# Sync-queue DMAs of an attention backward pass chained in traced order, with a third buffer for stored dV

## The chip, the cores and the metric

One core of a Trainium2 chip runs the whole program. The metric is device time in microseconds (us), the median of several executions. A ratio is the mean time of one kernel's runs over the mean of the other kernel's runs of the same rounds, so it is not quite the ratio of the medians that are quoted beside it.

## The reference, cut to what matters

Two independent blocks A and B each do attention of 96 queries on a cache of 512 keys and values, for 8 batches and 32 heads of width 128, in bf16. What is wanted is the output and the gradients of all inputs.

```python
def _A_ref(x, k_cache, v_cache, wq, wo):           # B=8, Sq=96, D=640, H=32, Sk=512, Dh=128
    q = (x @ wq).reshape(B, Sq, H, Dh).transpose(0, 2, 1, 3)
    scores = jnp.einsum("bhqd,bhkd->bhqk", q, k_cache) * (Dh ** -0.5)
    p = softmax(scores)
    o = jnp.einsum("bhqk,bhkd->bhqd", p, v_cache)
    return o.transpose(0, 2, 1, 3).reshape(B, Sq, H * Dh) @ wo
# ... B the same; concatenate([a, b], -1); then jax.vjp with grad_out for all ten inputs
```

For the argument it is enough that the kernel, for every (block, head, batch), reads K and V twice, once transposed and once as they lie, and writes a dK and a dV of the same size.

## The kernel before

The kernel is a software pipeline written by hand. One *tick* is one (head, batch). Each stage of the work is put on a list with a tick and a slot; the list is sorted and traced in that order. The framework's scheduler then orders the instructions of every engine by priority and readiness, so an engine's order can differ from the traced one.

Heads go in pairs (`HP = 2`): one DMA moves the K (or V, dK, dV) of two heads of one batch, 256 KB. There are 256 such *pairs*, one every two ticks, and each has six DMAs, all issued from the sync engine (SP): two transposing loads, two plain loads, two stores. The transposing loads are traced for two batches at once (`TB = 2`). I call the batches of such a couple *even* and *odd*.

```python
OFF = dict(t=-1, kn=3, vn=0, s2=3, s3=3, s4=4, s5=5, s6=6, s7=7, s8=8)
HP = 2
TB = 2
# ...
    def p_ldT(h, b, which):                       # transposing load of K (0) or V (1)
        def f():
            t_ = kvp.tile([128, F4 * KC, 16], BF16, name=key + "_p", bufs=(4 if which == 0 else 6))
            # ...
            nc.sync.dma_start_transpose(t_[:], src)                              # L246
    # p_ldn: plain load into K_sb / V_sb, bufs=4                                   L257
    def p_st(h, b, which):                        # store of dV (1) or dK (0)
        def f():
            t_ = CS[(blk, h, b)]["dV_p" if which == 1 else "dK_p"]
            dst = (dv if which == 1 else dk)[b, h:h + HP]
            nc.sync.dma_start(dst.rearrange("h (p c) d -> p h (c d)", c=KC), t_[:])   # L266
    # ...
    def c_s4(h, b):                               # dV = P^T dO, then a copy out of PSUM
        def f():
            # ... four matmuls into dV_ps
            if j == 0:
                st["dV_p"] = wk.tile([128, HP, KC * 128], BF16, name="dV_sb", bufs=2)
            nc.scalar.activation(dV_p[:, j], dV_ps[:], ACT.Identity, scale=1.0)  # L362
    # c_s7: the same for dK: dK_sb, bufs=2, copy on ScalarE                        L428
    # ...
                if j == 0:
                    if b % TB == 0:
                        for which in (0, 1):
                            for bb in range(b, b + TB):
                                em.add(ct + OFF["t"], SLOTS["LOAD"] - 1, p_ldT(h, bb, which))
                    em.add(ct + OFF["kn"], SLOTS["LOAD"], p_ldn(h, b, 0))
                    em.add(ct + OFF["vn"], SLOTS["LOAD"], p_ldn(h, b, 1))
                    em.add(ct + HP + OFF["s4"], SLOTS["LOAD"], p_st(h, b, 1))
                    em.add(ct + HP + OFF["s7"] + 1, SLOTS["LOAD"], p_st(h, b, 0))
```

## Time and profile before

Time 1757.6 us (three runs, 1757.0 to 1759.6).

| | before |
|---|---|
| TensorE (PE) busy | 1643 us, 93% |
| gaps between PE's instructions, summed (with the 6 us before the first) | 110 us |
| mean granted TensorE clock | 0.984 |
| DMA engines busy, all queues (87.7 + 8.4 + 0.7 + 0.1% of the span) | 1708 us of 1763 |
| ScalarE (ACT) copies waiting for a store, dK_sb / dV_sb | 24.5 / 23.3 us |

These lines are from the page of the kernel before. DMA is a row of 40 slices of the span in tenths; q1 is the sync queue and q0 the one issued by GpSimd, with packets, MB and share of the time of the 16 DMA engines; the last two lines are groups of instructions: count, busy us, mean ns, idle time just before them and what ended most of it.

```profile
span 1763.2 us, 59487 instructions
...
PE 1643.4 (93%) x22474; PEld 1371.8 (78%) x22648; DVE 1392.3 (79%) x3597; ACT 1349.2 (77%) x3529; POOL 712.9 (40%) x1306
...
DMA  9999999999999999999999999999999999999983
...
q1 hardware_dynamic: 304672, 404.75, 87.7%
q0 software_dynamic: 15648, 49.83, 8.4%
...
L428 ACT ACTIVATE dK_sb<-dK_ps 128x512 bf16<-128x512 f32 x512 | 302.6, 591 | 108.9 <-PE dK_ps L423 70.4
L362 ACT ACTIVATE dV_sb<-dV_ps 128x512 bf16<-128x512 f32 x512 | 307.8, 601 | 26.0 <-DMA out_dram<-dV_sb 23.3
```

TensorE and the DMA engines are both nearly full. The views that tell where PE loses time are the waits (total us, times, longest):

```profile
ACT dK_sb L428 <- DMA out_dram<-dK_sb: 24.5, 20, 3.3
...
ACT dV_sb L362 <- DMA out_dram<-dV_sb: 23.3, 16, 3.3
...
PE S_ps L286 <- ACT dK_sb L428: 18.1, 13, 3.3
```

A ScalarE copy into dK_sb or dV_sb sometimes finds its buffer still being stored (20 and 16 times); PE then waits for the copy, which empties a PSUM buffer (18.1 us at S_ps). The timeline of the sync queue (start, us, instruction) shows the order that the scheduler makes of one pair's six DMAs:

```profile
522.04 1.16 SPq L246 DMA_TRANSPOSE VT_p<-in_A_v_cache_dram  x1
523.29 0.53 SPq L266 DMA_DIRECT2D out_dram<-dV_sb  x1
523.91 1.82 SPq L246 DMA_TRANSPOSE KT_p<-in_A_k_cache_dram  x1
525.83 0.53 SPq L257 DMA_DIRECT2D V_sb<-in_A_v_cache_dram  x1
526.46 0.42 SPq L266 DMA_DIRECT2D out_dram<-dK_sb  x1
526.97 0.42 SPq L257 DMA_DIRECT2D K_sb<-in_A_k_cache_dram  x1
```

Transposes come in twos, often with a store between them, and a dK store is issued 2.4 us (median over the trace) after its data is ready. I call this time its *lag*.

### The profile page before, as it was taken

The numbers are of one execution on the slowest core, as the hardware profiler recorded it, in microseconds if no ns is written. First come the engines' busy times: TensorE is split into PE (matmuls) and PEld (weight loads), VectorE is DVE, ScalarE is ACT, GpSimd is POOL, SyncE is SP. The second block draws the span as 40 slices with busy tenths as digits, with TensorE's granted clock in tenths as the row PEclk, the third lists the DMA queues.
The fourth block names the chain that finished last, engine by engine and source line by source line (L and its number), as shares of the span: only waits on it lengthen the run. The fifth ranks groups of instructions, "written<-read, shape, count | busy, mean of one in ns | idle before, by whom it ended". The sixth has DMA issues, their size and how long they took to land. (4 is left out here: it accounts for less than half of the span.)

```text
span 1763.2 us, 59487 instructions
## 1 busy us (share of the span) xinstructions
PE 1643.4 (93%) x22474; PEld 1371.8 (78%) x22648; DVE 1392.3 (79%) x3597; ACT 1349.2 (77%) x3529; POOL 712.9 (40%) x1306
## 2 busy tenths in 40 slices
PE   5899989999999999998998999999999989999997
PEld 4787878788888888786886787877878878787776
DVE  4786868878888888887886778787888878888885
ACT  4888967878778787875876898786787867878782
POOL 3343434433433443434365344343443334343336
PEclk9899999999999999999999999999999999999999
DMA  9999999999999999999999999999999999999983
GB/s 267 262 280 258 265 251 262 270 261 273 266 266 284 264 268 257 273 271 259 242 278 282 262 268 273 249 268 252 264 265 269 262 239 265 267 269 246 263 249 111
DMA packets 320609, 458.39 MB, mean 260 GB/s; under 512 B 37216, under 2 KB 300896, under 8 KB 312128
## 3 DMA queue, kind: packets, MB, share of 16 engines
q1 hardware_dynamic: 304672, 404.75, 87.7%
q0 software_dynamic: 15648, 49.83, 8.4%
q8 instruction: 177, 2.90, 0.7%
q14 instruction: 112, 0.92, 0.1%
HBM read 161.09 MB, written 159.12 MB: 182 GB/s over the span
## 5 line engine op out<-in xcount | busy, mean ns | idle before, releaser
L298 ACT ACTIVATE E_sb<-S_ps,negm 96x512 bf16<-96x512 f32 x512 | 349.2, 682 | 212.6 <-DVE negm L288 203.6
L317 POOL TENSOR_SCALAR P_sb<-E_sb,rinv 96x512 bf16<-96x512 bf16 x512 | 354.2, 692 | 343.8 <-DVE rinv L308 339.4
L371 POOL TENSOR_TENSOR prod<-OT_h,dOT_h 128x96 bf16<-128x96 bf16 x512 | 188.1, 367 | 571.6 <-DVE OT_h L343 563.0
L385 DVE SCALAR_TENSOR_TENSOR dS_sb<-dP_ps,dl_ps,P_sb 96x512 bf16<-96x512 f32 x512 | 382.1, 746 | 35.4 <-PE dl_ps L383 22.4
L288 DVE TENSOR_REDUCE negm<-S_ps 96x1 f32<-96x512 f32 x512 | 347.9, 680 | 67.4 <-PE S_ps L286 66.6
L428 ACT ACTIVATE dK_sb<-dK_ps 128x512 bf16<-128x512 f32 x512 | 302.6, 591 | 108.9 <-PE dK_ps L423 70.4
L362 ACT ACTIVATE dV_sb<-dV_ps 128x512 bf16<-128x512 f32 x512 | 307.8, 601 | 26.0 <-DMA out_dram<-dV_sb 23.3
L346 ACT ACTIVATE PT_sb<-optp_ps 128x384 bf16<-128x384 bf16 x512 | 252.1, 492 | 0.9 <-PE optp_ps L340 0.5
L286 PE MATMUL S_ps<-KT_p,QT_h 128*96 128x512 bf16 x512 | 197.1, 385 | 18.6 <-ACT dK_sb L428 18.1
L357 PE MATMUL dV_ps<-dOnat_h,P_sb 96*128 96x128 bf16 x2048 | 200.4, 221 | 6.1 <-ACT dV_sb L362 6.1
L423 PE MATMUL dK_ps<-Qnat_h,dS_sb 96*128 96x128 bf16 x2048 | 199.9, 221 | 6.1 <-ACT dV_sb L362 5.8
L407 PE MATMUL dq_dst_ps<-ident,dS_sb 96*128 96x96 bf16 x2048 | 174.4, 208 | 27.9 <-DVE dS_sb L385 26.0
L381 PE MATMUL dP_ps<-VT_p,dOT_h 128*96 128x512 bf16 x512 | 197.3, 385 | 0.9 <-ACT dV_sb L362 0.9
L409 DVE COPY dST_sb<-dq_dst_ps 128x384 bf16<-128x384 bf16 x512 | 177.5, 347 | 15.3 <-PE dq_dst_ps L407 14.5
L333 PE MATMUL optp_ps<-PT_sb,V_sb 128*128 128x96 bf16 x2048 | 173.5, 207 | 5.2 <-ACT PT_sb L346 5.1
L340 PE MATMUL optp_ps<-ident,P_sb 96*128 96x96 bf16 x2048 | 173.4, 206 | 2.6 <-POOL P_sb L317 2.0
L400 PE MATMUL dq_dst_ps<-dST_sb,K_sb 128*128 128x96 bf16 x2048 | 172.9, 208 | 2.7 <-ACT dK_sb L428 2.5
L510 PE MATMUL o_ps<-wo_r,OT_h 128*128 128x256 bf16 (+1 forms) x1152 | 154.7, 259 | 1.4 <-ACT E_sb L298 0.3
L400 PEld LDWEIGHTS <-K_sb 128*128 128x128 bf16 x2048 | 135.9, 99 | 23.2 <-issue 3.6
L343 DVE CAST OT_h<-optp_ps 128x96 bf16<-128x96 f32 x512 | 126.8, 248 | 34.1 <-PE optp_ps L340 31.0
L510 PE MATMUL o_ps<-wqT_h,dQT_h 128*128 128x256 bf16 (+1 forms) x1152 | 150.4, 255 | 0.0
L308 DVE RECIPROCAL rinv<-rowsum 96x1 f32<-96x1 f32 x512 | 79.9, 156 | 87.5 <-ACT E_sb L298 65.8
(77 smaller groups left out, 3398.3 us busy)
## 6 DMA issues: line engine op xcount, KB each, us to landing
out_dram<-dV_sb SPq DMA_DIRECT2D x256, 256.0 KB, 4.1
out_dram<-dK_sb SPq DMA_DIRECT2D x256, 256.0 KB, 4.0
V_sb<-in_A_v_cache_dram SPq DMA_DIRECT2D x128, 256.0 KB, 4.0
K_sb<-in_A_k_cache_dram SPq DMA_DIRECT2D x128, 256.0 KB, 4.4
V_sb<-in_B_v_cache_dram SPq DMA_DIRECT2D x128, 256.0 KB, 4.0
K_sb<-in_B_k_cache_dram SPq DMA_DIRECT2D x128, 256.0 KB, 4.8
out_dram<-dwo_sb POOLq DMA_DIRECT2D x64, 160.0 KB, 5.0
out_dram<-dwq_sb POOLq DMA_DIRECT2D x32, 320.0 KB, 6.0
```

The costliest lines, as they stand in the source:

```text
L288: nc.vector.tensor_reduce(negm[:], S_ps[:], axis=AX.X, op=ALU.max, negate=True)
L298: nc.scalar.activation(E_sb[:].rearrange("q (a f) -> q a f", f=F4), st["S_ps"][:].rearrange("q (f a) -> q a f", f=F4), ACT.Exp, bias=st["n ...
L317: nc.gpsimd.tensor_scalar(P_sb[:], st["E_sb"][:], st["rinv"][:], 0.0, op0=ALU.mult, op1=ALU.add)
L346: nc.scalar.activation(PT_sb[:], PT_ps, ACT.Identity, scale=1.0)
L357: nc.tensor.matmul(dV_ps[:, c * 128:(c + 1) * 128], P_sb[:, c * 128:(c + 1) * 128], hs["dOnat_h"][:, b * 128:(b + 1) * 128], start=True, s ...
L362: nc.scalar.activation(dV_p[:, j], dV_ps[:], ACT.Identity, scale=1.0)
L381: nc.tensor.matmul(dP_ps[:], hs["dOT_h"][:, tok], st["VT"], start=True, stop=True)
L385: nc.vector.scalar_tensor_tensor(dS_sb[:].rearrange("q (a f) -> q a f", f=F4), dP_ps[:].rearrange("q (f a) -> q a f", f=F4), dl_ps[:, 0:1] ...
L400: nc.tensor.matmul(dQT_ps, st["K_sb"][:, c, :], st["dST_sb"][:, c * Sq:(c + 1) * Sq], start=(c == 0), stop=(c == KC - 1))
L423: nc.tensor.matmul(dK_ps[:, c * 128:(c + 1) * 128], dS_sb[:, c * 128:(c + 1) * 128], hs["Qnat_h"][:, b * 128:(b + 1) * 128], start=True, s ...
L428: nc.scalar.activation(dK_p[:, j], dK_ps[:], ACT.Identity, scale=1.0)
L510: nc.tensor.matmul(o_ps[:], src[:, t * 128:(t + 1) * 128], rhs, start=(hh == 0), stop=(hh == groups[g] - 1))
```

## The change

Every DMA of the sync queue goes through a `Chain`, which adds an ordering dependency on the one traced before it. The scheduler can no longer reorder them, so the four transposes traced together stay together. The hope is that transposes next to each other cost the DMA engines less. dV_sb gets a third buffer; `ob` and `ld_tmp` (pool `stp`) give one each to make room.

```diff
+class Chain:
+    def __call__(self, res):
+        ins = getattr(res, "ins", res)
+        if self.last is not None:
+            self.tc.add_manual_dep(ins, self.last.name, mybir.DependencyInfo(mybir.DependencyClass.NoSync, ...), reason="issue order")
+        self.last = ins
+        return res
...
-            nc.sync.dma_start_transpose(t_[:], src)
+            sp(nc.sync.dma_start_transpose(t_[:], src))
   (the same around the plain loads and the stores)
...
-                st["dV_p"] = wk.tile([128, HP, KC * 128], BF16, name="dV_sb", bufs=2)
+                st["dV_p"] = wk.tile([128, HP, KC * 128], BF16, name="dV_sb", bufs=3)
...
-                ob = wk.tile([128, w], BF16, name="ob", bufs=5)
+                ob = wk.tile([128, w], BF16, name="ob", bufs=4)
...
-                    em.add(ct + HP + OFF["s4"], SLOTS["LOAD"], p_st(h, b, 1))
-                    em.add(ct + HP + OFF["s7"] + 1, SLOTS["LOAD"], p_st(h, b, 0))
+                    em.add(ct + HP + OFF["s4"] + ST[0], SLOTS["LOAD"], p_st(h, b, 1))      # ST = (0, 1): no change
+                    em.add(ct + HP + OFF["s7"] + ST[1], SLOTS["LOAD"], p_st(h, b, 0))
...
-            stp=P(name="stp", bufs=3),
+            stp=P(name="stp", bufs=2),
```

More of the change, by code (lines that the diff above doesn't have):

```diff
@@ L46 @@
 TB = 2
+ST = (0, 1)
 HK = [
@@ L55, with __init__ @@
 SLOTS = dict(LOAD=0, S2A=5, S2B=5.5, S8=10, S7=20, S5=30, S4=40, S6=50, S3A=52, S3B=53, S5B=54, HEAD=SL_HEAD, GRP=SL_GRP)
+class Chain:
+    def __init__(self, tc):
+        self.tc = tc
+        self.last = None
+    def __call__(self, res):
+        ins = getattr(res, "ins", res)
+        if self.last is not None:
+            self.tc.add_manual_dep(ins, self.last.name, mybir.DependencyInfo(mybir.DependencyClass.NoSync, mybir.DependencyReason.DATA), reason="issue order")
+        self.last = ins
+        return res
 def build_block(tc, em, tick0, blk, x, kc, vc, wq, wo, g_all, out_all, dx, dk, dv, dwq, dwo, ident, ones, pools, HG=4, first=True, groups=None):
@@ L106, in build_block @@
     stp = pools["stp"]
+    sp = pools["sp"]
     def setup_ld(which_, c):
@@ L256, in f @@
             src = (kc if which == 0 else vc)[b, h:h + HP]
-            nc.sync.dma_start(t_[:].rearrange("p h c d -> p h (c d)"), src.rearrange("h (p c) d -> p h (c d)", c=KC))
+            sp(nc.sync.dma_start(t_[:].rearrange("p h c d -> p h (c d)"), src.rearrange("h (p c) d -> p h (c d)", c=KC)))
             for j in range(HP):
@@ L265, in f @@
             dst = (dv if which == 1 else dk)[b, h:h + HP]
-            nc.sync.dma_start(dst.rearrange("h (p c) d -> p h (c d)", c=KC), t_[:])
+            sp(nc.sync.dma_start(dst.rearrange("h (p c) d -> p h (c d)", c=KC), t_[:]))
             if which == 0:
@@ L519, in f @@
             else:
-                ob = wk.tile([128, w], BF16, name="ob", bufs=5)
+                ob = wk.tile([128, w], BF16, name="ob", bufs=4)
                 nc.vector.tensor_tensor(ob[:], o_ps[:], acc[:, t, c0:c0 + w], op=ALU.add)
@@ L619, in _kernel_impl @@
             grp=P(name="grp", bufs=1),
-            stp=P(name="stp", bufs=3),
+            stp=P(name="stp", bufs=2),
         )
+        pools["sp"] = Chain(tc)
         pools["S45"] = {}
```

## The prediction

> **What bounds the kernel now.** Mainly TensorE: the page's busy table gives PE 1643 of 1763 us (93%); the windows view gives 95 to 96.6% in good stretches of 100 us. PE's gaps sum to 110 us. About 26 lie in the first 100 us, about 26 are a repeating 1.5 us wait of dS transposes on DVE, and much of the rest comes from stores: the waits view shows ACT's dK copies waiting 24.5 us (20 times) and its dV copies 23.3 us (16 times) for the store that still reads their buffer; PE then waits about 36 us in all for those copies (S_ps 18.1). Halved-clock stretches of 3.4 to 6.8 us follow 12 to 15 us after most longer PE stalls, about 25 us lost in all.
>
> The DMA engines look full (DMA row 9 everywhere, queue table 87.7 + 8.4%), but not with bytes. In the packet records a plain 1 KB packet takes 46 ns. A transposing packet (16 KB, one on each of 16 engines) takes 0.73 us at best and 1.33 on average; those of one transpose start up to 5 us apart and end nearly together, so early engines wait for late ones. [...] That alignment wait is 512 x 0.6 = 307 us of every engine. A transpose directly behind another mostly takes 0.8 to 0.95.
>
> **What the change does.** Now the timeline of SP shows per head pair and batch V-transpose, K-transpose, dV, dK, V, K, often with a store between the transposes. After: per two batches KKVV transposes, then eight plain ones. First of four about 1.5 to 1.9 us, the others 0.85 to 0.95: about 4.4 against 5.3 us, so about 110 us less DMA busy time per engine (estimate from the packets). No bytes change.
>
> Cost: stores queue behind four transposes. They take SP about 6 us to issue (1.1, 1.7, 2.1, 1.2 in the early quadruple at 18 to 24 us). The dK store of the odd batch stands behind them and a K load: it now issues 2.3 us (median) after its data is ready; I estimate 4, against 8.5 us from ready to reuse and a 4 us landing. So dK waits of odd batches may grow from 24 towards 30 us or more; dK of even batches improves. The third buffer gives dV about 6.5 us more: its 23 us of waits should vanish. Loads are safe: K transposes issue 12.5 us or more before use.
>
> Two buffers taken away: ld_tmp 3 to 2 lengthens the waits at the block change (6.3 us now at 814 to 841) by about 5 us; ob 5 to 4 adds 1 to 3 us.
>
> **Sum.** Removed: dV-derived PE waits about 14 us, part of the dK ones about 8, halved clock about 8. Added: about 7 at the block change and end, a few for odd dK. Net about -18 us.
>
> Prediction 1739 us, 8 in 10 between 1712 and 1772. Faster by over 2% 0.20, within 2% 0.69, slower 0.11.
>
> **What would show it.** Transposing packets' mean 1.05 to 1.15 us; q1 share down from 87.7% to 80 to 83%; SP timeline with four transposes in a row; no ACT dV_sb wait on its store; dK_sb waits 15 to 35 us, on odd batches; ld_tmp waits about 10 us; fewer halved-clock stretches.
>
> **What would make it wrong.** If odd dK stores land late every time (a microsecond each 13 us), the kernel loses 50 us or more. If freed DMA time makes all stores land early, all 36 us and most clock losses go: about 1710.

## The result, and the profile after

1967.4 us (four runs, 1965.3 to 1970.3) against 1758.6 us (the three runs above and a fourth of 1767.2): the ratio is 1.118, 95% interval 1.114 to 1.122. The change costs 12%, far outside the predicted range.

| | before | after |
|---|---|---|
| span of the profiled run | 1763.2 | 1963.5 |
| PE busy | 1643.4 | 1708.9 |
| gaps between PE's instructions | 110 | 243 |
| of these, gaps over 2 us | 32 (8 gaps) | 163 (45 gaps) |
| mean granted clock | 0.984 | 0.947 |
| DMA engines busy (mean of the 16, from the packet records) | 1709 | 1670 |
| DMA engines idle (the rest of the span) | 54 | 293 |

The 200 us consist of 133 us more gaps and 66 us more PE busy time. The second goes with the lower clock: (1 - 0.947) x 1963.5 minus (1 - 0.984) x 1763.2 is 76 us of lost clock. The order of PE's instructions is exactly the same in both kernels, and that of ScalarE nearly, so nothing of this is a rescheduled computation. The same lines of the page after (line numbers are 17 higher):

```profile
span 1963.5 us, 58982 instructions
...
PE 1708.9 (87%) x22474; PEld 1414.8 (72%) x22648; DVE 1404.3 (72%) x3597; ACT 1354.0 (69%) x3529; POOL 713.2 (36%) x1306
...
DMA  9998889888799888888789978898898978888783
...
q1 hardware_dynamic: 304672, 404.75, 76.8%
q0 software_dynamic: 15648, 49.83, 7.5%
...
L445 ACT ACTIVATE dK_sb<-dK_ps 128x512 bf16<-128x512 f32 x512 | 303.1, 592 | 276.5 <-DMA out_dram<-dK_sb 204.4
...
L379 ACT ACTIVATE dV_sb<-dV_ps 128x512 bf16<-128x512 f32 x512 | 308.1, 602 | 0.6 <-PE dV_ps L374 0.6
```

The dV_sb waits are gone, as intended. The dK_sb copies wait 204 us for their store, eight times as long as before, and PE waits behind them:

```profile
ACT dK_sb L445 <- DMA out_dram<-dK_sb: 204.4, 74, 5.4
...
PE nat_ps L458 <- ACT dK_sb L445: 105.3, 28, 4.9
```

The sync queue itself waited most for this, in the waits view of the SP queue, before and after:

```profile
SPq L266 <- ACT dV_sb L362: 37.6, 86, 2.8
...
SPq L283 <- ACT dV_sb L379: 348.6, 124, 6.2
```

By this view a store stood at the head of the queue 124 times, 2.8 us on average, until a copy into dV_sb was done. The SP queue's own times say more plainly where: in front of the even batches' dV stores it issued nothing for 441 us in all (127 of 128 stores), before the change for 13 us (22 stores). I call this the queue's *stand*. The following piece of the timelines shows one turn: first the sync queue after the change, then ScalarE, then PE.

```profile
498.31 0.38 SPq L283 DMA_DIRECT2D out_dram<-dV_sb  x1
498.79 0.42 SPq L274 DMA_DIRECT2D V_sb<-in_A_v_cache_dram  x1
499.26 3.60 SPq L263 DMA_TRANSPOSE KT_p<-in_A_k_cache_dram  x2
502.91 3.14 SPq L263 DMA_TRANSPOSE VT_p<-in_A_v_cache_dram  x2
506.09 0.58 SPq L274 DMA_DIRECT2D K_sb<-in_A_k_cache_dram  x1
506.77 0.41 SPq L283 DMA_DIRECT2D out_dram<-dK_sb  x1
```

```profile
497.68 0.60 ACT L379 ACTIVATE dV_sb<-dV_ps 128x512 bf16<-128x512 f32 x1
...
505.29 0.49 ACT L363 ACTIVATE PT_sb<-optp_ps 128x384 bf16<-128x384 bf16 x1
510.67 0.60 ACT L445 ACTIVATE dK_sb<-dK_ps 128x512 bf16<-128x512 f32 x1 [4.89 <-DMA out_dram<-dK_sb]
```

```profile
506.70 0.16 PE L400 MATMUL dl_ps<-ones,prod 128*96 128x1 bf16 x1
511.32 0.80 PE L458 MATMUL nat_ps<-ident,dQT_h 128*128 128x128 bf16 x6 [4.45 <-ACT dK_sb L445]
```

The copy into dV_sb ends at 497.68 + 0.60 = 498.28, and at 498.31 its store is issued, which had held the queue. Then come a load, the four transposes (499.26 to 506.05) and a load, and only at 506.77 the store of the odd batch's dK. ScalarE wants that buffer back at about 505.8, waits 4.89 us and copies at 510.67, when the store has landed. PE stands still for 4.45 us.

Over the whole trace, from the starts and ends of these instructions: the odd batch's dK store is issued 5.5 us (median) after its data is ready, the even batch's 1.3 us; before, 2.3 and 2.4. Of the 204 us that ScalarE waits for dK stores, 201 fall on odd batches; before, 4.4 of the 24.5 did. The median steps of a turn are 0.95 us from the dV store to the first transpose, 5.9 us to issue the four, 1.1 us to the end of the dK store's issue, and 4.8 us to the copy that reuses the buffer.

### The profile page after: what moved, and what is told of

It reads as the page before. It is cut to its first block, busy times and chain, and to the rows that moved or that the text cites. A ratio compares the mean times of both kernels' runs of the same rounds, so it can differ in the third digit from the quotient of the medians.

```text
span 1963.5 us, 58982 instructions
## 1 busy us (share of the span) xinstructions
PE 1708.9 (87%) x22474; PEld 1414.8 (72%) x22648; DVE 1404.3 (72%) x3597; ACT 1354.0 (69%) x3529; POOL 713.2 (36%) x1306
## 3 DMA queue, kind: packets, MB, share of 16 engines
q1 hardware_dynamic: 304672, 404.75, 76.8%
## 5 line engine op out<-in xcount | busy, mean ns | idle before, releaser
L445 ACT ACTIVATE dK_sb<-dK_ps 128x512 bf16<-128x512 f32 x512 | 303.1, 592 | 276.5 <-DMA out_dram<-dK_sb 204.4
L303 PE MATMUL S_ps<-KT_p,QT_h 128*96 128x512 bf16 x512 | 202.2, 395 | 11.4 <-ACT dK_sb L445 9.1
L424 PE MATMUL dq_dst_ps<-ident,dS_sb 96*128 96x96 bf16 x2048 | 177.0, 210 | 26.4 <-DVE dS_sb L402 24.5
L527 PE MATMUL o_ps<-wo_r,OT_h 128*128 128x256 bf16 (+1 forms) x1152 | 162.6, 268 | 1.1
L473 PE MATMUL dwo_ps<-g_nat,Onat 128*128 128x128 bf16 (+1 forms) x704 | 136.7, 313 | 22.3 <-ACT dK_sb L445 18.7
```

The source lines that it names most:

```text
L303: nc.tensor.matmul(S_ps[:], hs["QT_h"][:, tok], st["KT"], start=True, stop=True)
L445: nc.scalar.activation(dK_p[:, j], dK_ps[:], ACT.Identity, scale=1.0)
```

## The experiments

Theory A: the odd batch's dK store stands behind the four transposes and lands after its buffer is wanted again, because dK has two buffers. Rival B: four transposes in a row hold up the queue and the DMA engines as such, loads included. Rival C: the queue's in-order stand in front of stores whose data is not there is what costs, wherever the dK store is. All kernels of the experiments gave correct results.

### x1: the third buffer on dK in place of dV

```diff
-name="dV_sb", bufs=3      -name="dK_sb", bufs=2
+name="dV_sb", bufs=2      +name="dK_sb", bufs=3
```

> The changed kernel with its third buffer moved from the stored dV to the stored dK; same SBUF, same order of the sync queue, four transposes in a row. Theory A (the store of the odd batch's dK, which stands behind the four transposes, lands about 10 us after its data is ready where two buffers leave 8.5 us, and the ScalarE copy into dK_sb waits): the dK_sb waits of 204 us vanish, time 1735 to 1790 us. Theory B (four transposes in a row hold up the DMA engines and the sync queue, so everything on it is late, loads too): little changes, 1930 to 1970 us. Theory C (it is the sync queue standing still for a dV store whose data is not yet there): dV with two buffers is still issued first, so also 1930 or more.

Measured: 1793.9 us, ratio 1.016 (1.011 to 1.020). That is 4 us above theory A's range. The same 2 KB of SBUF per partition, spent on the other tensor, take away 0.102 of the 0.118. ScalarE's two groups of copies, in the listing of instruction groups with all releasers of their idle time:

```profile
L379 ACT ACTIVATE dV_sb<-dV_ps 128x512 bf16<-128x512 f32 x512 | 307.5, 601 | 106.5 <-DMA out_dram<-dV_sb 96.8 <-PE dq_dst_ps L417 3.9 <-PE S_ps L303 1.7
L445 ACT ACTIVATE dK_sb<-dK_ps 128x512 bf16<-128x512 f32 x512 | 302.4, 591 | 84.3 <-PE dK_ps L440 81.0
```

The dK waits on stores are gone (their rest is waiting for PE), though the odd batch's dK store is now issued even later, 8.8 us after its data. The dV copies with two buffers wait 97 us. Four transposes still stand in a row, and the order of the queue is unchanged. B and C, which both forecast 1930 us or more, fall as the main cause, and A holds; that dV came to wait was not expected. The stand before the even batches' dV stores fell as well, from 441 to 93 us, so most of it was fed by the late dK copies; x5 below shows the other direction, so the two drive each other round a loop.

### x2: the chain left out, the buffers kept

```diff
-        if self.last is not None:
+        if False:
```

> The changed kernel with the chain of dependencies left out: the order of the sync queue is the scheduler's again, but three dV buffers, ob 4 and ld_tmp 2 stay. All theories say that the loss comes from the order: 1735 to 1765 us. If the buffers taken from ob and ld_tmp caused the loss: over 1900 us. My prediction's part for the third dV buffer alone: ACT's dV_sb waits on its store (23.3 us before) fall under 3 us and the time falls by 10 to 20 us against before.

Measured: 1769.7 us, ratio 1.003 (0.998 to 1.007). The time is 5 us above my range. The order is the cause of the loss, not the buffers taken from ob and ld_tmp. It also tests my prediction's gain of 10 to 20 us from dV. In the waits, dV_sb copies wait for no store, but the dK_sb copies wait 43.1 us in place of 24.5:

```profile
ACT dK_sb L445 <- DMA out_dram<-dK_sb: 43.1, 28, 3.9
```

Most of the time that the dV buffer saves comes back as waits of the next tensor in the same queue, and nothing is gained. (The buffers given up add a little: PE waits 9.3 us for ld_tmp against 6.3, VectorE 15.9 for ob against 13.2.)

### x3: chained, but transposes traced in twos

```diff
-TB = 2
+TB = 1
```

> The changed kernel, still chained in traced order, but the transposes traced per batch (two in a row every two ticks, in place of four every four). Theory A: the dK store stands behind two transposes, about 3.5 us less, so lag after its data about 2 us and no waits of weight: 1740 to 1800 us. Theory B (row of four): 1740 to 1800 us too. Theory C (in-order waits on a dV store): every second tick the queue stands still as before, 1900 us or more.

Measured: 1845.3 us, ratio 1.044 (1.037 to 1.051). Between the theories: there are now mostly two transposes in front of the dK store of every batch. Its lag is 4.4 us (odd) and 4.8 (even), the dK_sb waits are 119 us in 80 waits, on both kinds of batches alike. I had expected a lag of 2 us; a shorter row takes away more than half of the loss, but not all of it as long as the order forces every dK store behind one.

### x4: chained, four in a row, the dK store traced before them

```diff
-ST = (0, 1)
+ST = (0, 0)
-        em.add(ct + OFF["t"], SLOTS["LOAD"] - 1, p_ldT(h, bb, which))
+        em.add(ct + OFF["t"], SLOTS["LOAD"] + 1, p_ldT(h, bb, which))
```

(The release of the program's bookkeeping for the pair stays one tick later.)

> The changed kernel, chained, four transposes still in a row, but each dK store one tick earlier and the transposes traced after the other DMAs of their tick, so that the odd batch's dK store goes out before the four transposes. Theory A: dK_sb waits under 20 us, 1725 to 1780 us, unless the transposes now come too late for S_ps. Theory B (row of four): over 1900 us. Theory C (queue waits for stores' data): over 1900 us, because the queue now waits for dK as well as dV.

Measured: 1785.2 us, ratio 1.008 (1.001 to 1.015; one of the four runs was 1763.1). The sync queue shows the odd dK store ahead of the row:

```profile
513.37 0.38 SPq L283 DMA_DIRECT2D out_dram<-dK_sb  x1
513.84 0.42 SPq L274 DMA_DIRECT2D K_sb<-in_A_k_cache_dram  x1
514.31 4.24 SPq L263 DMA_TRANSPOSE KT_p<-in_A_k_cache_dram  x2
518.59 2.48 SPq L263 DMA_TRANSPOSE VT_p<-in_A_v_cache_dram  x2
```

```profile
L382 ACT ACTIVATE dV_sb<-dV_ps 128x512 bf16<-128x512 f32 x512 | 308.0, 602 | 1.7 <-PE dV_ps L377 1.7
L448 ACT ACTIVATE dK_sb<-dK_ps 128x512 bf16<-128x512 f32 x512 | 302.9, 592 | 150.9 <-PE dK_ps L443 84.7 <-DMA out_dram<-dK_sb 56.0 <-ACT PT_sb L366 4.9
```

The odd batch's lag is 0.03 us, and 56 us of dK waits are left, now all on even batches (lag 3.5 us), whose stores come behind the row. So A's own forecast, under 20 us of waits and at most 1780 us, was just missed. With the same chain, the same four in a row and the same two dK buffers, moving the dK stores by one tick and the transposes by two slots removes nine tenths of the loss. This is the strongest evidence for A against B. It also speaks against C: SP stood still in front of stores for 195 us in x4 and for 143 us in x3 (520 in the changed kernel), and yet x4 is the faster of the two.

### x5: the dV stores one tick later

```diff
-ST = (0, 1)
+ST = (1, 1)
```

> The changed kernel with every dV store traced one tick later, so that the even batch's dV store follows the four transposes in the queue where it preceded them; everything else as changed. It asks whether the queue's stand in front of that store (348 us in 124 waits on the dV copies) starts the loop: if that stand is a real link (theory A with the dV copy as the loop's start), the transposes go out 2 to 3 us earlier, the dK store's median lag in odd batches falls from 5.5 to about 3 us and the time to 1780 to 1870 us. If only the issue time of the four transposes and what gates them (the K buffer that S_ps frees) counts, the wait moves to the transposes and the time stays at 1930 to 1975 us.

Measured: 1863.8 us, ratio 1.062 (1.056 to 1.067); odd lag 4.2 us, where I expected about 3, and dK_sb waits 125.6 us. The stand before the even batch's dV store is gone, and half of the loss with it, so it is a real link. (The edit moves the odd batches' dV stores too; no run separates the two.) The dK store is still behind the row, and part of the stand has only moved: SP now stands 166 us in front of the second transpose (10 in the changed kernel). The waits view of SP has the transposes (L263) waiting for PE now; its largest entry:

```profile
SPq L263 <- PE optp_ps L350: 108.2, 28, 5.0
```

### x6: the chain alone, dV back at two buffers

```diff
-name="dV_sb", bufs=3
+name="dV_sb", bufs=2
```

> The changed kernel with the dV buffers back at two: the chain alone (ob 4 and ld_tmp 2 kept). In the changed kernel dV stores issue at once in even batches and 1.6 us late in odd ones, and with one buffer less some 8.8 us would still be left to land in; theory A says dV is not in the loop's last link: 1955 to 1990 us, dV_sb waits under 30 us. If the third dV buffer kept something much worse away: over 2000 us.

Measured: 1962.9 us, ratio 1.112 (1.106 to 1.118); dK_sb waits 208.8 us and no dV_sb waits on a store. The third dV buffer does nothing in the changed kernel.

### x7: chained, three buffers for both

```diff
-name="dK_sb", bufs=2      -name="ob", bufs=4
+name="dK_sb", bufs=3      +name="ob", bufs=3
```

> The changed kernel with a third buffer for dK too (ob 3 in place of 4 to make room), chained, four in a row. Theory A: no ACT waits for stores at all, 1730 to 1775 us, about as fast as before or a little faster. If the order has a further cost beyond the stores' buffers: 1790 us or more.

Measured: 1804.6 us, ratio 1.027 (1.024 to 1.031). Worse than expected, and not better than x1. 59 us of dK_sb waits are left, although a third buffer is there: the whole queue runs later (odd lag 10.4 us; the issue of a K transpose ends 12.2 us before its use, against 17.8 in the changed kernel). This asked for x13 and x14.

### x8: not chained, three buffers for both

```diff
 (the kernel before)
-name="dV_sb", bufs=2   -name="dK_sb", bufs=2   -bufs=(4 if which == 0 else 6)   -name="ob", bufs=5
+name="dV_sb", bufs=3   +name="dK_sb", bufs=3   +bufs=(4 if which == 0 else 5)   +name="ob", bufs=4
```

> The kernel before, without the chain, with three buffers for dV and for dK (V transposes 5 buffers in place of 6, ob 4 in place of 5 to make room). x2 has shown that three dV buffers alone take away the 23 us of dV waits but that the dK waits grow from 24.5 to 43 us and the time stays. Theory A: with both, no ACT waits for stores; time 1715 to 1745 us, 1 to 2.5% under before. If the block change or DMA holds the kernel instead: 1750 to 1765 us.

Measured: 1722.3 us (1721.1 to 1723.4), ratio 0.980 (0.976 to 0.983). It beats both kernels, the one before by 2%. Lines of its page, and its two groups of copies in the listing:

```profile
span 1721.6 us, 59658 instructions
...
PE 1641.8 (95%) x22648; PEld 1365.3 (79%) x22648; DVE 1389.0 (81%) x3597; ACT 1345.0 (78%) x3529; POOL 713.2 (41%) x1306
...
DMA  9999999999999999999899999999999999999982
...
q1 hardware_dynamic: 304672, 404.75, 89.0%
q0 software_dynamic: 15648, 49.83, 8.2%
```

```profile
L362 ACT ACTIVATE dV_sb<-dV_ps 128x512 bf16<-128x512 f32 x512 | 307.9, 601 | 5.5 <-DMA out_dram<-dV_sb 1.7 <-PE S_ps L286 1.4 <-PE dV_ps L357 1.3
L428 ACT ACTIVATE dK_sb<-dK_ps 128x512 bf16<-128x512 f32 x512 | 302.5, 591 | 80.9 <-PE dK_ps L423 71.6 <-DMA out_dram<-dK_sb 6.5
```

ScalarE waits 8 us in all for stores, in place of 48. The DMA engines are now busy for 98.0% of the span (89.0 + 8.2 + 0.7 + 0.1).

### x9: x4 with a third dK buffer

```diff
 (x4)
-name="dK_sb", bufs=2   -name="ob", bufs=4
+name="dK_sb", bufs=3   +name="ob", bufs=3
```

> x4 (chained, dK store traced before the four transposes) with a third dK buffer as well (ob 3). Theory A: the 56 us of dK_sb waits of x4 vanish and the time falls from 1785 to 1725 to 1755 us.

Measured: 1775.0 us, ratio 1.011 (1.006 to 1.015), no better than x4. The dK_sb waits do vanish (7 us), but PE now waits 21.5 us for K transposes that land too late, where the other kernels show under 1 us of that. A miss of the forecast: putting the row last moves the lateness to the loads.

### x10 and x11: only the loads chained

```diff
-            sp(nc.sync.dma_start(dst.rearrange("h (p c) d -> p h (c d)", c=KC), t_[:]))
+            nc.sync.dma_start(dst.rearrange("h (p c) d -> p h (c d)", c=KC), t_[:])
 (x11 also: dK_sb bufs=3, ob bufs=3)
```

> The changed kernel with only the loads chained (transposes and plain loads in traced order); the 512 stores are left to the scheduler, which puts them between the transposes. It asks whether it is the stores' place in the queue, and the queue's stand in front of stores whose data is not there, that cost the time. Theory: DMA idle time per engine (293 us of the span in the changed kernel, 54 before) falls under 110 us, dK_sb waits under 70 us, time 1750 to 1800 us. If the loads' own order costs: over 1850 us.

> x10 with a third dK buffer (ob 3). So far every kernel keeps a DMA engine busy for 1670 to 1709 us and differs in the idle time; x8 (scheduler's order, both third buffers) is at 1722 us with 33 us idle. If pairs of transposes side by side save DMA time at all, this one is below x8: 1700 to 1720 us. If adjacency is worth nothing (mean packet 1.3 us in rows of four too): 1720 to 1760 us.

Measured: x10 1854.5 us, ratio 1.049 (1.042 to 1.056); x11 1759.1 us, ratio 0.996 (0.991 to 1.001). x10 is a miss: I took it that a free store would be placed well, but the scheduler still puts the dK store behind two or three transposes (odd lag 3.8 us, dK_sb waits 125.5 us). With a third dK buffer most of it disappears. x11 is not below x8, nor below x13 (0.992, below), which has the same buffers and no chain, so transposes side by side save nothing that shows in the time.

### x12: not chained, the third buffer on dK only

```diff
 (x2)
-name="dV_sb", bufs=3   -name="dK_sb", bufs=2
+name="dV_sb", bufs=2   +name="dK_sb", bufs=3
```

> x2 with the third buffer on dK in place of dV: scheduler's order, dV 2, dK 3, ob 4, ld_tmp 2. It fills the square of x2 (dV alone: 1.003), x8 (both: 0.980). If either third buffer only moves the wait to the other store, as x2 showed (dV waits 23 to 0, dK waits 24 to 43 us): dK_sb waits 0, dV_sb waits 35 to 60 us, 1745 to 1775 us. If dK was the wait that counted: 1720 to 1740 us.

Measured: 1791.7 us, ratio 1.011 (1.004 to 1.018). The dK_sb waits on stores vanish, the dV_sb waits rise to 64 us, a little more than the 35 to 60 I expected. With x2 this shows that one third buffer only moves the wait to the other store. The time is even above my range.

### x13 and x14: the chain's own share when both have three buffers

x13 is x7 without the chain (`if False:`), x14 is the changed kernel with the buffers of x8 (dK_sb 3, V transposes 5, ob 4, stp 3), that is x8 with the chain.

> x7 without the chain (three buffers for dV and dK, ob 3, ld_tmp 2, scheduler's order). If the chain is what x7 pays for: about as x8, 1725 to 1745 us (0.98 to 0.99 of before), dK_sb waits under 15 us. If ob 3 and ld_tmp 2 are: 1780 us or more.

> x8 with the chain and four transposes in a row (three buffers for dV and dK, V transposes 5, ob 4, ld_tmp 3). If the in-order queue itself costs because it stands still in front of stores whose data is not there, while the DMA engines have no time to spare (x8 keeps them busy for 98% of the span): DMA idle over 90 us and 1785 to 1815 us. If the buffers were the cost in x7: 1725 to 1750 us.

Measured: x13 1754.6 us, ratio 0.992 (0.988 to 0.996), just above my range; x14 1788.3 us, ratio 1.012 (1.006 to 1.018), inside it.

| buffers dV / dK, others | scheduler's order | chained |
|---|---|---|
| 2 / 3, ob 4, ld_tmp 2 | 1.011 (x12) | 1.016 (x1) |
| 3 / 2, ob 4, ld_tmp 2 | 1.003 (x2) | 1.118 (the change) |
| 3 / 3, ob 3, ld_tmp 2 | 0.992 (x13) | 1.027 (x7) |
| 3 / 3, ob 4, ld_tmp 3, V transposes 5 | 0.980 (x8) | 1.012 (x14) |

With three buffers for both, the chain costs 3 to 4%; with three for dV and two for dK, 11.5%; with two for dV and three for dK, nothing clear of noise. Between the two lower rows, which differ in the buffers that pay for the third ones, lies 1 to 2%; in the kernels with ob 3 (x7, x9, x11, x13) VectorE waits 27 to 30 us for ob, in the others 13 to 19. The DMA engines of x14 are idle for 88 us, those of x8 for 33.

Across all kernels the packets keep a DMA engine busy for 1670 to 1712 us, whatever the order; what differs is how long they are idle. With so little to spare (33 us idle in x8, 54 before), I took a stand of the queue that lets them run dry for lost time. That the chained queue's waits for dV data cause the remaining 3% is a reading that fits, but no run isolates it, so it stays argued. x14 also still shows 60 us of dK_sb waits, nearly all for the stores of odd batches (with three buffers it is an even batch's copy that waits for them).

### Lag and waits side by side

Median time from a dK pair being ready to the issue of its store, in the kernels with two dK buffers:

| | odd lag, us | even lag, us | dK_sb waits, us | ratio |
|---|---|---|---|---|
| before | 2.3 | 2.4 | 24.5 | 1 |
| x4 | 0.03 | 3.5 | 56.0 | 1.008 |
| x3 | 4.4 | 4.8 | 119.0 | 1.044 |
| x10 | 3.8 | 1.6 | 125.5 | 1.049 |
| x5 | 4.2 | 0.1 | 125.6 | 1.062 |
| x6 | 5.3 | 1.3 | 208.8 | 1.112 |
| after | 5.5 | 1.3 | 204.4 | 1.118 |

The longer lag of the two goes with the waits and the time.

## Why the prediction was wrong

**The step that failed** is the sentence "I estimate 4, against 8.5 us from ready to reuse and a 4 us landing. So dK waits of odd batches may grow from 24 towards 30 us or more". The place was right, odd batches behind four transposes; the size was not. In odd batches the lag is 5.5 us, and the store lands 4.25 us after its issue starts (before 3.9). From data ready to store landed it takes 10.0 us (median of the pairs) where I had 8, and ScalarE is back for the buffer after 9.3 us (median; 9.2 before, where I had 8.5). In 77 of 127 turns the store had not landed by then; 70 of these show as waits, 2.9 us on average. My numbers left half a microsecond, which is no margin for a queue whose times spread over several microseconds (in one turn of ten the store lands more than 12 us after its data is ready). The waits came to 204 us where I had some 30, and my starting point was wrong too: of the 24 us before, only 4.4 were on odd batches. The last section of the prediction names this very case, at "50 us or more", as an unlikely one; x1 and x4 show that it was the main effect.

**Why the lag was 5.5 and not 4.** I let the four transposes start when their K buffer comes free. In the chained order they also wait for the even batch's dV store in front of them, and that store for its data (441 us in 127 stands). In these stands SP issued nothing, 3.5 us a time: a store that was not ready held back what stood behind it. x5 measures the link: with that store behind the row, half of the loss goes.

**With PE's gaps came halved clock.** I expected fewer stretches of halved clock. The clock records show 10 before and 42 after, 60 and 209 us in all, each with a granted share of 0.5, so half of that time is lost. I also placed them "12 to 15 us after" the stalls, which was an error: I compared two time bases that are some 10.7 us apart. The windows view of the kernel before shows where one of the long ones lies; PE stood still from 238.9 to 241.6 us.

```profile
core 0: us, PE busy (x) PEld busy (x) DVE busy (x) ACT busy (x) POOL busy (x), PEclk, DMA share, GB/s
233.00:241.00 8.00, 4.39 (x59) 3.62 (x56) 4.17 (x11) 3.05 (x10) 2.08 (x4) 0.99 0.92 261
241.00:248.00 7.00, 6.41 (x57) 5.26 (x57) 3.95 (x11) 3.90 (x11) 1.06 (x2) 0.53 0.92 267
```

In the clock record the stretch begins at 240.8 us, shortly before that gap ends, and lasts 6.8 us. After the change 41 of the 42 stretches begin during a gap of 1.8 us or longer, or within 1.6 us of its end. My runs show that gaps and halved clock go together; that the one causes the other is not shown.

**Transposes side by side.** The alignment that I had read from the packets is there; the gain did not come. The packets of one transpose end close together (the median spread of their ends is 0.09 us before), and a transpose's mean packet time follows the spread of its packets' starts (correlation 0.88 before). But "those of one transpose start up to 5 us apart" was wrong: I had mixed in the instruction-fetch packets of the same size (177 of them); the median spread of the starts is 0.6 us, and 1.2 for the first of a pair (3.5 at the most). The term that was mis-sized is "the others 0.85 to 0.95". Mean packet times by place in the row:

| | 1st | 2nd | 3rd | 4th | sum, us |
|---|---|---|---|---|---|
| before (two pairs) | 1.54 | 1.17 | 1.53 | 1.07 | 5.32 |
| x1 (four in a row, DMA engines idle for 97 us) | 1.73 | 1.13 | 1.25 | 1.22 | 5.34 |
| after (four in a row, DMA engines idle for 293 us) | 1.24 | 1.29 | 1.25 | 1.17 | 4.95 |

The pairs of before already had the saving of a second transpose, though often a store stood between the two. In the rows of four the third and fourth cost 1.2 us and not 0.9; with nearly full engines (x1) the first costs more. Per engine the transposes take 681 us before, 683 in x1, 664 in x4 and 633 after: at most 47 us where I had 110, and none in x1, where the engines are nearly full. The share of q1 did fall, to 76.8%, but mostly because the span grew: its busy time went from 1546 to 1508 us. The issue of a transpose takes SP 1.2 us after the change (median; 1.3 before), which may be what paces the third and fourth; that is argued, not tested.

**What held.** The dV_sb waits vanished and the dK waits of even batches shrank (from 20.1 to 3.1 us), but the gain I booked for them (14 us and some clock) did not come even without the chain: in x2 the dK waits grew from 24.5 to 43.1 us. The waits for ld_tmp (8.2 us after, 6.3 before) and ob (14.4 after, 13.2 before) grew by little, as forecast. The loads were safe in the changed kernel: PE waits for no K or V transpose there.

## What to carry to other kernels

The sync queue, once held in order, passed its waits on to what stood behind (441 us of stands in front of the even batches' dV stores), so before fixing a queue's order, follow each buffer round its loop: data ready, place in the queue, issue, landing, next use; and ask for a margin as large as the spread of those times. Where several tensors take turns in a queue as full as here (the DMA engines were busy for 1709 of 1763 us), give a further buffer to all of them (dV and dK together here: 0.980, or 0.992 where ob and ld_tmp paid for it), since one alone may only hand the wait to the next (1.003 and 1.011). And count in what may come with a stall: after the change 41 of the 42 stretches at half the clock, each 3.4 or 6.8 us long, began in or just after a gap of 1.8 us or longer on TensorE.

## What the traces show of transposing DMAs

- The fastest twentieth of the transposing packets take 0.73 us or less (16 x 16 KB in 0.73 us is 359 GB/s), but in a stream mixed with copies they take 1.33 us on average, 197 GB/s; the same 16 KB as plain 1 KB packets take 16 x 0.051 = 0.82 us (before).
- The 16 engines' parts of one transpose end together (median spread 0.09 us) however far apart they start (median 0.6, at most 3.5 us), so that a packet that starts early takes longer; the packets of the second transpose of a pair have a median of 0.82 us, those of the first 1.47 (before).
- The issue of a transposing DMA takes SP 1.1 us at the least and 1.75 us on average before the change, 1.46 after, against 0.52 and 0.53 for a plain one; four transposes take the sync queue 5.9 us (median, after).
